# One reader for two PSUM banks: merged maxima and exponentials, and a third pair of W2 tiles split early

## The chip, the core and the metric

The kernel runs on one core of a Trainium2 chip. Its engines are TensorE (PE in the profile, with its weight loads listed apart as PEld), VectorE (DVE), ScalarE (ACT), GpSimd (POOL) and SyncE (SP, which here only issues DMAs). Each engine takes its instructions in the order of the program and waits on semaphores. The metric is the device time of one execution in microseconds (us).

## What is computed

```python
x = A_x                                             # [1, 2048, 576], float32
g = sigmoid((x * gate_w).sum(-1, keepdims=True))
# a: attention, 32 heads of 18 dimensions
q, k, v = split(x @ wqkv)
p = softmax(einsum("bhqd,bhkd->bhqk", q, k) * 18 ** -0.5)
a = concat(p @ v) @ wo
# b: MLP, 576 -> 4608 -> 576
h = gelu(layernorm(x) @ w1 + b1)                    # tanh form
b = h @ w2 + b2
out = g * a + (1 - g) * b
```

## The kernel before

The program has three parts. An **entry stage** loads x, normalises and transposes it, multiplies it with `wqkv`, and starts on the attention's maxima. A **loop** of 512 steps follows: 32 units (a pair of heads times one half of the 2,048 queries), each with 16 chunks of 128 keys. The **end** multiplies the attention's output with `wo` and adds the MLP's part.

Most float32 matrices are split into a high and a low part that TensorE multiplies as fp32r, so that products keep float32 accuracy. Heads come in pairs: head 0 lies in rows 0 to 63 of the array, head 1 in rows 64 to 127, and two matmuls of 64 rows that follow each other run side by side.

Each step of the loop holds, in the order in which the Python code emits it:

- two **S pairs** (`s2`, L263): for each head one matmul (L271) of 128 keys against 512 queries into a PSUM bank of its own, and for each head one exponential on ScalarE (L275) from that bank into the probabilities' ring (`p`, `ring`).
- two **R pairs** (`s1_round`, L216), for a unit that comes more than one unit later: for each head one matmul (L226) of 128 queries against 512 keys into a bank of its own, and one maximum over the row on VectorE (L228), which the later exponentials of that unit subtract through two more rows of the matmul.
- every two or three steps, `pv` (L280): the matmuls of probabilities and values (L291) for these steps.
- between them, pieces of the **MLP** (`atom`, L743): its hidden product (L539, `h_pair`) and its output product (L627, `out_pair`). `turn_ends` cuts one `h_pair` or one `out_pair` into the gaps between two calls of `pv`; below such a stretch is called a turn.

PSUM has eight banks of 512 float32 columns. In the loop the scores use five of them in turn (`score_bank`, L117: three of the pool `ps_s1` and two of `ps_s2`), the output of `pv` has one, and the MLP two. S and R pairs alternate, so the five banks go round through both. A matmul that reuses a bank waits for the instruction that read the bank last: ScalarE's exponential or VectorE's maximum.

The MLP's weights are read from the input once, split by ScalarE (L402 to L405, the high part) and GpSimd (through `pool_op`, L179, the low part), used, and stored to scratch; the later three blocks of 512 rows reload them. `prep` and `prep_w2` (L436, L450) ask for these splits ahead of time; `bg` holds them until their input is due (`LOADED`, a number of slots after the load was issued) and GpSimd's modelled queue is short. There are six W2 tiles (`room`), two for each pair of F chunks. Before, the entry stage asks for the first two pairs (`prep_w2(2)`, L688), and the others follow in the loop (L726).

Of the kernel before, what the change touches and what calls it, by code (L numbers as in the profile page):

```python
# [8 lines left out]
F32 = mybir.dt.float32  # L9
# [25 lines left out]
HALF = S // 2  # L35
NS1 = 3
LEAD = 4
# [29 lines left out]
def gated_mix_kernel(ctx: ExitStack, tc: tile.TileContext, x, wqkv, wo, w1, b1, w2, b2, gate_w, out):  # L67
# [34 lines left out]
    asm = ctx.enter_context(tc.tile_pool(name="asm", bufs=2))  # L102
    ps_s1 = ctx.enter_context(tc.tile_pool(name="ps_s1", bufs=NS1, space=PSUM))
    ps_o = ctx.enter_context(tc.tile_pool(name="ps_o", bufs=1, space=PSUM))
    QA = [att.tile([P, HALF], F32R, name=f"qa{i}") for i in range(3)]
# [5 lines left out]

    def psum(pool):
        return pool.tile([P, TB], F32, name="ps")

    ring = [0]

    def score_bank():  # L117

        ring[0] += 1
        if not looped[0]:  # L120
            return psum(ps_s1 if ring[0] % (NS1 + 1) < NS1 else ps_o)
        return psum(ps_s1 if ring[0] % (NS1 + 2) < NS1 else ps_s2)

# [92 lines left out]
    def s1_round(u, r):  # L216


        t, kb = (r % 8, r // 8) if u in (0, NU - 3) else divmod(r, 4)
        if r == 0:  # L220
            M4[u] = asm.tile([P, 2, 8, 4], F32, name="m4")
        qa, ka = QA[u % 3], KA[unit(u)[0] % 2]
        for h in range(2):
            r0 = 64 * h
            ps = score_bank()
            nc.tensor.matmul(ps, qa[r0:r0 + 54, t * P:(t + 1) * P], ka[r0:r0 + 54, kb * TB:(kb + 1) * TB],  # L226
                             start=True, stop=True)
            nc.vector.tensor_reduce(M4[u][:, h, t, kb:kb + 1], ps, axis=AX.X, op=ALU.max)  # L228

# [33 lines left out]
    def s2(u, kc, qb):  # L263
        qa, ka = QA[u % 3], KA[unit(u)[0] % 2]
        n = u * NT + kc
        if n < 2 and qb == 0:
            RING.insert(n, pp.tile([P, 2, 2, TB], F32, name="p"))
        ps = [score_bank() for _ in range(2)]
        for h in range(2):
            r0 = 64 * h  # L270
            nc.tensor.matmul(ps[h], ka[r0:r0 + 56, kc * P:(kc + 1) * P], qa[r0:r0 + 56, qb * TB:(qb + 1) * TB],  # L271
                             start=True, stop=True)
        def exps():
            for h in range(2):
                nc.scalar.activation(p_of(n)[:, qb, h], ps[h], AF.Exp, scale=SCALE)  # L275
        return exps
# [3 lines left out]
    def pv(n, m):  # L280

        u, kc = divmod(n, NT)
        if kc == 0:
            OB[u] = psum(ps_o)
# [55 lines left out]
    def mlp():  # L340
# [26 lines left out]
        def load_w1(q):  # L367

            if (1, q) in LOADED or q >= NQ0:
                return  # L370
            LOADED[1, q] = slot[0] + LAND
            f0 = 2 * q * P
            raw = raw1(q)
            for h in range(2):
                src = w1[256 * h:256 * h + 256, f0:f0 + 2 * P].rearrange("(c p) n -> p c n", p=64)
                nc.sync.dma_start(raw[64 * h:64 * h + 64, 0:8].rearrange("p (c j) n -> p c (j n)", j=2), src)
            for h in range(2):
                for j in range(2):
# [135 lines left out]
        def h_pair(q, inner=False):  # L514
# [8 lines left out]
            del W1[q]  # L523
            ps = [psum(ps_w) for _ in range(2)]
            change = tb + 1 < NB and (q + 1) % NQ0 == 0
# [78 lines left out]
        def out_pair(i, t, acc):  # L604
# [3 lines left out]
            cs = [slice(nn * ND, (nn + 1) * ND) for nn in range(2)]  # L608
            ps = [psum(ps_w) for _ in range(2)]
            steps = 12 * size  # L610
# [77 lines left out]
        prep_w2(2)  # L688
        prep(2)
        yield 1  # L690
        Y[1] = big_tile()
# [18 lines left out]
        for i in range(n + 1):  # L710
# [3 lines left out]
            if i > 0:  # L714
# [55 lines left out]
    with ExitStack() as a:  # L770
        wpool = a.enter_context(tc.tile_pool(name="a_w", bufs=1, side="right"))
        sm = a.enter_context(tc.tile_pool(name="a_sm", bufs=2, side="right"))
        ps_a = a.enter_context(tc.tile_pool(name="ps_a", bufs=4, space=PSUM))

# [45 lines left out]
        def transposed(tb, c):  # L820
            ps = psum(ps_a)
# [67 lines left out]
        def stat_rows(tb):  # L889

            ps = psum(ps_a)
            nc.tensor.transpose(ps[:, :P], stp, ident)
# [46 lines left out]
        def qk_group(tb, mt):  # L939
            big = xT[tb]  # L940
            wh, wl = W_QK
            ms = slice(mt * P, (mt + 1) * P)
            ps = psum(ps_a)
            k = 0
# [14 lines left out]
        def v_group(tb, t, n, between=None):  # L959
# [3 lines left out]
            wh, wl = W_V  # L963
            ps = psum(ps_a)
            k = 0
# [38 lines left out]
        for tb in range(NB):  # L1004
            work = [(qk_group, (tb, mt)) for mt in (range(9) if tb < 2 else (4, 0, 1, 2, 3, 5, 6, 7, 8))] + [(v_group, (tb, t, n)) for t in range(4) for n in range(2)]
            for g, (fn, args) in enumerate(work):
# [35 lines left out]
                if tb == NB - 1:  # L1042
# [12 lines left out]
                    if g == 7:  # L1055
                        ps = psum(ps_a)
                        nc.tensor.transpose(ps[:, :NFC], b1r, ident[:NFC, :NFC])
# [19 lines left out]

    ps_s2 = ctx.enter_context(tc.tile_pool(name="ps_s2", bufs=2, space=PSUM))
    ps_w = ctx.enter_context(tc.tile_pool(name="ps_w", bufs=2, space=PSUM))
    cw = ctx.enter_context(tc.tile_pool(name="c_w", bufs=1, side="right"))  # L1080
# [9 lines left out]
    def out_proj():  # L1090
# [171 lines left out]
        for b in range(NB):  # L1262
# [6 lines left out]
            for t in range(4):  # L1269
# [6 lines left out]
                for n in range(2):  # L1276
                    cs = slice(n * ND, (n + 1) * ND)
                    ps = psum(ps_w)
                    k = 0
# [127 lines left out]
```

## Time and profile before

| | us |
|---|---|
| Median of 3 runs | 2239.05 (2237.3 to 2239.54) |
| The profiled execution | 2238.79, its span 2237.0 |
| Entry stage, to the first S pair | 216.4 |
| Granted TensorE clock, mean | 0.994 |

| In the loop and around it (whole run) | instructions | mean ns of one |
|---|---|---|
| Maxima on VectorE, L228 | 2048 | 684 |
| Exponentials on ScalarE, L275 | 1048 + 1000 | 597 and 596 |
| R matmuls, L226 | 2048 | 403 |
| S matmuls, L271 | 2048 | 421 |
| Hidden product, L539 | 3888 | 393 |
| Output product, L627 | 6912 in four groups | 294 to 299 |

A group's line reads: source line, engine, operation, out<-in by the program's names, the shape, the count, then busy time, mean of one in ns, and the engine's idle time just before these instructions with what ended most of it. A line of the timeline reads: start, length (from the first start to the last end of merged neighbours), engine, line, operation, names, shape, count, and in brackets the idle time before it. Two matmuls of a pair overlap, so a pair's length of 0.40 us to 0.50 us is not the sum of the two.

### The profile page before, as it was taken

The page shows a single profiled execution, that of the slowest core. Times are in us where ns is not written, and L with a number is a line of the kernel's source. Part 1 is how long each engine was busy: PE and PEld are TensorE (multiplying, and loading weights), DVE is VectorE, ACT ScalarE, POOL GpSimd, SP SyncE. Part 2 cuts the span into 40 slices and gives each one's busy share as a digit, 9 for nine tenths or more (in the row PEclk, how much of TensorE's full clock was granted, in tenths as well). Part 3 has the DMA queues.
Part 4 walks back from the last instruction along what each step waited for, and adds up shares of the span by engine and source line. Part 5 has one row for each costly group of instructions (what it writes and reads, how often), then busy time and mean ns, then how long its engine had stood idle before and what let it go on. Part 6 is the DMA issues. An engine that isn't in the chain of part 4 may idle for free.

```text
span 2237.0 us, 51358 instructions
## 1 busy us (share of the span) xinstructions
PE 2204.4 (99%) x20496; PEld 1620.0 (72%) x20496; DVE 1619.0 (72%) x2816; ACT 1418.5 (63%) x2636; POOL 1005.0 (45%) x1017
## 2 busy tenths in 40 slices
PE   8999999999999999999999999999999999999999
PEld 7877666767677777777767677777677777777768
DVE  6675766777777777777777777777777777777734
ACT  4323866767776666666765676666666666667672
POOL 4322765556554525434543452543535354254600
PEclk9999999999999999999999999999999999999999
DMA  8857646444453522342341533243344324323355
GB/s 265 273 205 240 216 149 191 148 152 157 145 166 120 181 101 97 125 138 94 125 138 58 171 142 111 91 141 125 107 131 156 118 85 150 110 91 124 124 171 167
DMA packets 162041, 324.36 MB, mean 145 GB/s; under 512 B 65830, under 2 KB 85218, under 8 KB 151074
## 3 DMA queue, kind: packets, MB, share of 16 engines
q1 hardware_dynamic: 159494, 317.61, 44.1%
q8 instruction: 161, 2.64, 0.5%
q10 hardware_dynamic: 2244, 3.45, 0.4%
q14 instruction: 78, 0.64, 0.1%
q0 software_dynamic: 64, 0.02, 0.0%
HBM read 228.62 MB, written 96.69 MB: 145 GB/s over the span
## 4 chain that ended last, share of the span: by engine, by line
PE 86%; DMA 4%; DVE 4%; POOL 2%; issue 2%; SPq 1%; ACT 1%; POOLq 0%; ACTq 0%; DVEq 0%
PE ps L291 19%; PE ps L627 19%; PE ps L539 18%; PE ps L271 12%; PE ps L226 10%; PE ps L947 3%; PE ps L1284 2%; DVE m L228 2%; DMA x<-in_B_w_dram 1%; PE ps L968 1%; POOL zz L179 1%; POOL w L179 1%; DMA bt<-b_scr 1%; SPq L380 1%; DMA x<-ot_scr 0%
## 5 line engine op out<-in xcount | busy, mean ns | idle before, releaser
L228 DVE TENSOR_REDUCE m<-ps 128x1 f32<-128x512 f32 x2048 | 1302.5, 684 | 450.7 <-PE ps L226 428.8
L275 ACT ACTIVATE p<-ps 128x512 f32<-128x512 f32 x1048 | 567.5, 597 | 305.8 <-PE ps L271 277.3
L275 ACT ACTIVATE ring<-ps 128x512 f32<-128x512 f32 x1000 | 542.4, 596 | 273.1 <-PE ps L271 263.7
L539 PE MATMUL ps<-big,w 64*128 64x512 f32 x3888 | 612.7, 393 | 0.2 <-issue 0.2
L179 POOL TENSOR_SCALAR zz<-zz 128x512 f32<-128x512 f32 x288 | 178.2, 619 | 726.3 <-ACT zz L599 670.9
L271 PE MATMUL ps<-qa,ka 56*128 56x512 f32 x2048 | 474.2, 421 | 6.7 <-ACT ring L275 3.0
L226 PE MATMUL ps<-ka,qa 54*128 54x512 f32 x2048 | 461.1, 403 | 7.4 <-DVE m L228 7.3
L539 PEld LDWEIGHTS ps<-big,w 64*128 64x128 f32 x3888 | 412.1, 187 | 51.4 <-DMA big<-y_scr 0.5
L179 POOL TENSOR_TENSOR zz<-zz,z 128x512 f32<-128x512 f32 x288 | 371.2, 1289 | 24.0
L271 PEld LDWEIGHTS ps<-qa,ka 56*128 56x128 f32 x2048 | 220.8, 185 | 198.2 <-DVE m L228 124.0
L627 PE MATMUL ps<-w,hh 64*128 64x288 f32 x2752 | 317.9, 296 | 1.2 <-DMA w<-w_scr 1.2
L627 PEld LDWEIGHTS ps<-w,hh 64*128 64x128 f32 x2752 | 277.8, 188 | 15.7 <-POOL zz L179 1.0
L226 PEld LDWEIGHTS ps<-ka,qa 54*128 54x128 f32 x2048 | 245.9, 185 | 39.0 <-DVE m L228 14.2
L291 PE MATMUL ps<-p,vt 128*32 128x512 f32 x1968 | 240.7, 597 | 0.0
L627 PE MATMUL ps<-w,big 64*128 64x288 f32 x2496 | 234.0, 294 | 3.4 <-ACT w L405 2.5
L627 PE MATMUL ps<-w,hl 64*128 64x288 f32 x1376 | 233.1, 294 | 0.0
L291 PE MATMUL ps<-ring,vt 128*32 128x512 f32 x1872 | 231.3, 596 | 0.0
L627 PEld LDWEIGHTS ps<-w,big 64*128 64x128 f32 x2496 | 218.7, 188 | 13.9 <-ACT w L405 2.8
L179 POOL TENSOR_TENSOR w<-x,w 128x1024 fp32r<-128x1024 f32 (+1 forms) x72 | 101.3, 1429 | 211.7 <-ACT w L402 120.2
L627 PEld LDWEIGHTS ps<-w,hl 64*128 64x128 f32 x1376 | 159.3, 187 | 0.2
L291 PEld LDWEIGHTS ps<-p,vt 128*32 128x32 f32 x1968 | 54.5, 109 | 116.3 <-issue 107.9
L291 PEld LDWEIGHTS ps<-ring,vt 128*32 128x32 f32 x1872 | 52.5, 109 | 115.1 <-issue 115.1
(126 smaller groups left out, 1715.8 us busy)
## 6 DMA issues: line engine op xcount, KB each, us to landing
w<-w_scr SPq DMA_DIRECT2D x54, 1152.0 KB
w<-w_scr SPq DMA_DIRECT2D x108, 576.0 KB
w_scr<-w SPq DMA_DIRECT2D x18, 1152.0 KB
w_scr<-w SPq DMA_DIRECT2D x36, 576.0 KB
qa<-qk_scr SPq DMA_DIRECT2D x192, 72.0 KB
ka<-qk_scr SPq DMA_DIRECT2D x84, 144.0 KB
x<-in_B_w_dram SPq DMA_DIRECT2D x36, 288.0 KB
qk_scr<-hh SPq DMA_DIRECT2D x36, 256.0 KB
```

What stands on the lines that cost most here:

```text
L179: fn(*args, **kw)
L226: nc.tensor.matmul(ps, qa[r0:r0 + 54, t * P:(t + 1) * P], ka[r0:r0 + 54, kb * TB:(kb + 1) * TB], start=True, stop=True)
L228: nc.vector.tensor_reduce(M4[u][:, h, t, kb:kb + 1], ps, axis=AX.X, op=ALU.max)
L271: nc.tensor.matmul(ps[h], ka[r0:r0 + 56, kc * P:(kc + 1) * P], qa[r0:r0 + 56, qb * TB:(qb + 1) * TB], start=True, stop=True)
L275: nc.scalar.activation(p_of(n)[:, qb, h], ps[h], AF.Exp, scale=SCALE)
L291: nc.tensor.matmul(OB[u][r:r + 32, :], v[:, k, 19 * h:19 * h + 32], p_of(c)[:, qb, h, :], start=(k == 0), stop=(k == NT - 1))
L380: nc.sync.dma_start(raw[64 * h:64 * h + 64, 8 + j], w1[512:576, f1:f1 + P])
L539: mm = nc.tensor.matmul(ps[nn], w_[r, 2 * c + nn if c < 4 else 8], y, start=(k == 0), stop=(k == 26))
L627: mm = nc.tensor.matmul(ps[nn][:, :ND], h_[r, tok], w_[p_][r, cs[nn]], start=(k == 0), stop=(k == steps - 1))
L947: nc.tensor.matmul(ps, w_[:, c, ms], big[:, s_, :], start=(k == 0), stop=False)
L968: nc.tensor.matmul(ps[:, :ND], big[:, s_, tok], w_[:, c, cs], start=(k == 0), stop=False)
L1284: nc.tensor.matmul(ps[:, :ND], OT[b][2][:, s_, tok], w_part(w_, c)[:, cs], start=(k == 0), stop=(k == 13))
```

## The change

All PSUM is now one tile `PS` of eight banks, and tables say which banks a use goes round through: in the loop "s" is 0 to 4, "w" (the MLP) 6 and 7, "o" (`pv`) 5. `score_banks` takes two banks at once and tells whether they lie side by side. If so, one VectorE instruction takes both heads' maxima and one ScalarE instruction both heads' exponentials; if not, there are two as before. With five banks the pairs are (0,1), (2,3), (4,0), (1,2), (3,4): every fifth pair is read by two instructions. In the entry stage "s" is (0, 1, 2, 5), so every second pair is.

```diff
-    ps_s1 = ctx.enter_context(tc.tile_pool(name="ps_s1", bufs=NS1, space=PSUM))
-    ps_o = ctx.enter_context(tc.tile_pool(name="ps_o", bufs=1, space=PSUM))
+    PS = ctx.enter_context(tc.tile_pool(name="ps", bufs=1, space=PSUM)).tile([P, 8, TB], F32, name="ps")
...
+    BANKS = {"s": (0, 1, 2, 5), "a": (3, 4, 6, 7), "o": (5,), "w": (6, 7)}
+    given = {}
+    def bank(use):
+        given[use] = given.get(use, -1) + 1
+        return BANKS[use][given[use] % len(BANKS[use])]
+    def score_banks():
+        pair = (bank("s"), bank("s"))
+        if pair[1] == pair[0] + 1:
+            return [PS[:, b] for b in pair], [(slice(0, 2), PS[:, pair[0]:pair[1] + 1])]
+        return [PS[:, b] for b in pair], [(slice(h, h + 1), PS[:, b:b + 1]) for h, b in enumerate(pair)]
...
+        ps, reads = score_banks()
         for h in range(2):
             r0 = 64 * h
-            ps = score_bank()
-            nc.tensor.matmul(ps, qa[r0:r0 + 54, t * P:(t + 1) * P], ka[r0:r0 + 54, kb * TB:(kb + 1) * TB],
+            nc.tensor.matmul(ps[h], qa[r0:r0 + 54, t * P:(t + 1) * P], ka[r0:r0 + 54, kb * TB:(kb + 1) * TB],
                              start=True, stop=True)
-            nc.vector.tensor_reduce(M4[u][:, h, t, kb:kb + 1], ps, axis=AX.X, op=ALU.max)
+        for hs, banks in reads:
+            nc.vector.tensor_reduce(M4[u][:, hs, t, kb], banks, axis=AX.X, op=ALU.max)
...
-            for h in range(2):
-                nc.scalar.activation(p_of(n)[:, qb, h], ps[h], AF.Exp, scale=SCALE)
+            for hs, banks in reads:
+                nc.scalar.activation(p_of(n)[:, qb, hs], banks, AF.Exp, scale=SCALE)
...
+    BANKS["s"] = (0, 1, 2, 3, 4)
+    given["s"] = -1
```

The second part concerns W2: the entry stage asks for a third pair of tiles, a load that is issued in the loop counts as landed four slots later than before, and at a block's end the reloads are one slot apart, no longer two.

```diff
-            LOADED[1, q] = slot[0] + LAND
+            LOADED[1, q] = slot[0] + LAND + 4 * looped[0]
...
-            LOADED[2, c] = slot[0] + LAND
+            LOADED[2, c] = slot[0] + LAND + 4 * looped[0]
...
-        def prep_w2(upto):
+        def prep_w2(upto, apart=2):
...
-                    late += 2
+                    late += apart
...
         prep_w2(2)
         prep(2)
+        prep_w2(3)
...
-                    prep_w2(first_of[i] + seq[i][2] + 2 * (seq[i][0] == 0 and not last_of(i)))
+                    prep_w2(first_of[i] + seq[i][2] + 2 * (seq[i][0] == 0 and not last_of(i)), 1 if last_of(i) else 2)
```

TensorE's instructions stand in the same order before and after. On VectorE, early in the loop, twelve R pairs stand between an eviction of the hidden product (`z`) and the end of a unit's maxima (`nm`). Before:

```order
L564 TENSOR_SCALAR z<-ps,b1t 128x512
L228 TENSOR_REDUCE m_2125<-ps 128x1 x16
L564 TENSOR_SCALAR z<-ps,b1t 128x512
L228 TENSOR_REDUCE m_2125<-ps 128x1 x8
L235 TENSOR_REDUCE nm<-m_2125 128x16
```

and now, at the same place:

```order
L569 TENSOR_SCALAR z<-ps,b1t 128x512
L233 TENSOR_REDUCE m_1951<-ps 128x2
L233 TENSOR_REDUCE m_1951<-ps 128x1 x2
L233 TENSOR_REDUCE m_1951<-ps 128x2 x4
L233 TENSOR_REDUCE m_1951<-ps 128x1 x2
L233 TENSOR_REDUCE m_1951<-ps 128x2
L569 TENSOR_SCALAR z<-ps,b1t 128x512
L233 TENSOR_REDUCE m_1951<-ps 128x2 x3
L233 TENSOR_REDUCE m_1951<-ps 128x1 x2
L240 TENSOR_REDUCE nm<-m_1951 128x16
```

Nothing has moved past anything else; of 12 pairs here nine have one reduction with two results (128x2) and three still have two. On ScalarE, behind an eviction of the hidden product (`z`) early in the loop, before:

```order
L565 ACTIVATE z<-ps,b1t 128x512
L275 ACTIVATE ring_2367<-ps 128x512 x2
L599 ACTIVATE zz<-z 128x512 x2
L402 ACTIVATE w_2947<-x 128x1152
L403 ACTIVATE w_2947<-x 128x128
L275 ACTIVATE ring_2367<-ps 128x512 x2
L275 ACTIVATE ring_2371<-ps 128x512 x4
L275 ACTIVATE p<-ps 128x512 x2
```

and now:

```order
L570 ACTIVATE z<-ps,b1t 128x512
L280 ACTIVATE ring_2161<-ps 128x1024
L604 ACTIVATE zz<-z 128x512 x2
L407 ACTIVATE w_2622<-x 128x1152
L408 ACTIVATE w_2622<-x 128x128
L280 ACTIVATE ring_2161<-ps 128x512 x2
L280 ACTIVATE ring_2165<-ps 128x1024 x2
L280 ACTIVATE p<-ps 128x1024
```

Again the order is the same, and an exponential now has 1,024 columns wherever the pair's banks are neighbours. On SP's queue, at the change from the entry stage to the loop (`v_scr` is a store of the entry, `x<-in_B_w` a load of raw weights, `w_scr` a store of split ones), before:

```order
L982 DMA v_scr<-vt_111 128x780
L376 DMA x<-in_B_w_dram 64x4x256 x2
L380 DMA x<-in_B_w_dram 64x128 x4
L414 DMA w_scr<-w_2453 128x2304
```

and now:

```order
L987 DMA v_scr<-vt_109 128x780
L391 DMA x<-in_B_w_dram 128x576 x2
L419 DMA w_scr<-w_2184 128x1152
L381 DMA x<-in_B_w_dram 64x4x256 x2
L385 DMA x<-in_B_w_dram 64x128 x4
L419 DMA w_scr<-w_2234 128x2304
```

Two loads of W2 and a store of a split W2 tile (128x1152) have moved ahead of the next W1 load; the store of the other tile follows later.

More of the change, by code (lines that the diff above doesn't have):

```diff
@@ L35 @@
 HALF = S // 2
-NS1 = 3
 LEAD = 4
@@ L110, in gated_mix_kernel, with psum @@
     oe = att.tile([P, TB], F32, name="oe")
[L112 to L122, printed above, removed]
+    BANKS = {"s": (0, 1, 2, 5), "a": (3, 4, 6, 7), "o": (5,), "w": (6, 7)}
[3 more added lines that the diff above has]
+        return BANKS[use][given[use] % len(BANKS[use])]
+    def psum(use):
+        return PS[:, bank(use)]
+    def score_banks():
[3 more added lines that the diff above has]
+        return [PS[:, b] for b in pair], [(slice(h, h + 1), PS[:, b:b + 1]) for h, b in enumerate(pair)]
     def big_tile():
@@ L267, in s2 @@
             RING.insert(n, pp.tile([P, 2, 2, TB], F32, name="p"))
-        ps = [score_bank() for _ in range(2)]
+        ps, reads = score_banks()
         for h in range(2):
@@ L283, in pv @@
         if kc == 0:
-            OB[u] = psum(ps_o)
+            OB[u] = psum("o")
         v = v_of(unit(u)[0])
@@ L523, in h_pair @@
             del W1[q]
-            ps = [psum(ps_w) for _ in range(2)]
+            ps = [psum("w") for _ in range(2)]
             change = tb + 1 < NB and (q + 1) % NQ0 == 0
@@ L608, in out_pair @@
             cs = [slice(nn * ND, (nn + 1) * ND) for nn in range(2)]
-            ps = [psum(ps_w) for _ in range(2)]
+            ps = [psum("w") for _ in range(2)]
             steps = 12 * size
@@ L772, in gated_mix_kernel @@
         sm = a.enter_context(tc.tile_pool(name="a_sm", bufs=2, side="right"))
-        ps_a = a.enter_context(tc.tile_pool(name="ps_a", bufs=4, space=PSUM))
         qkstack = ExitStack()
@@ L820, in transposed @@
         def transposed(tb, c):
-            ps = psum(ps_a)
+            ps = psum("a")
             for t in range(4):
@@ L889, in stat_rows @@
         def stat_rows(tb):
-            ps = psum(ps_a)
+            ps = psum("a")
             nc.tensor.transpose(ps[:, :P], stp, ident)
@@ L942, in qk_group @@
             ms = slice(mt * P, (mt + 1) * P)
-            ps = psum(ps_a)
+            ps = psum("a")
             k = 0
@@ L963, in v_group @@
             wh, wl = W_V
-            ps = psum(ps_a)
+            ps = psum("a")
             k = 0
@@ L1055, in gated_mix_kernel @@
                     if g == 7:
-                        ps = psum(ps_a)
+                        ps = psum("a")
                         nc.tensor.transpose(ps[:, :NFC], b1r, ident[:NFC, :NFC])
@@ L1075, in gated_mix_kernel @@
                     run_due()
-    ps_s2 = ctx.enter_context(tc.tile_pool(name="ps_s2", bufs=2, space=PSUM))
-    ps_w = ctx.enter_context(tc.tile_pool(name="ps_w", bufs=2, space=PSUM))
+    BANKS["s"] = (0, 1, 2, 3, 4)
+    given["s"] = -1
     cw = ctx.enter_context(tc.tile_pool(name="c_w", bufs=1, side="right"))
@@ L1277, in out_proj @@
                     cs = slice(n * ND, (n + 1) * ND)
-                    ps = psum(ps_w)
+                    ps = psum("w")
                     k = 0
```

## The prediction

> **What bounds the kernel now.** I read the page's first part, then the groups, then the timeline of TensorE (PE) beside VectorE (DVE) and ScalarE (ACT), because the change touches the two engines that empty PSUM and leaves TensorE's order of matmuls as it is.
>
> ```profile
> span 2237.0 us, 51358 instructions
> PE 2204.4 (99%) x20496; PEld 1620.0 (72%) x20496; DVE 1619.0 (72%) x2816; ACT 1418.5 (63%) x2636; POOL 1005.0 (45%) x1017
> ```
>
> TensorE is busy for 99% of the span; VectorE and ScalarE have room. Less work on those two is therefore worth nothing by itself. What counts is only whether TensorE waits for them, and for that the idle column of the groups is the place.
>
> ```profile
> L228 DVE TENSOR_REDUCE m<-ps 128x1 f32<-128x512 f32 x2048 | 1302.5, 684 | 450.7 <-PE ps L226 428.8
> L275 ACT ACTIVATE p<-ps 128x512 f32<-128x512 f32 x1048 | 567.5, 597 | 305.8 <-PE ps L271 277.3
> L271 PE MATMUL ps<-qa,ka 56*128 56x512 f32 x2048 | 474.2, 421 | 6.7 <-ACT ring L275 3.0
> L226 PE MATMUL ps<-ka,qa 54*128 54x512 f32 x2048 | 461.1, 403 | 7.4 <-DVE m L228 7.3
> L627 PE MATMUL ps<-w,big 64*128 64x288 f32 x2496 | 234.0, 294 | 3.4 <-ACT w L405 2.5
> L539 PE MATMUL ps<-big,w 64*128 64x512 f32 x3888 | 612.7, 393 | 0.2 <-issue 0.2
> ```
>
> The score matmuls (L271 for the exponentials, L226 for the maxima) idle for 6.7 + 7.4 = 14.1 us in the whole run. That is all that an earlier release of banks could give back. The more telling question is how near the banks are to being late. A hand-over shows it:
>
> ```profile
> 374.83 0.68 DVE L228 TENSOR_REDUCE m<-ps 128x1 f32<-128x512 f32 x1
> 375.56 0.18 PEld L271 LDWEIGHTS ps<-qa,ka 56*128 56x128 f32 x1 [1.09 <-DVE m L228]
> 375.57 0.50 PE L271 MATMUL ps<-qa,ka 56*128 56x512 f32 x1 [0.76 <-DVE m L228]
> ```
>
> The reduction ends at 375.51, the waiting weight load starts 0.05 us later, and its matmul ends at 376.07: **0.55 us** from the end of the reader to the end of the matmul that reuses the bank. TensorE stands still meanwhile.
>
> **The change part by part.** *The merged instructions.* The ring has five banks and each pair of scores takes two. The second bank of a pair was the first bank of the pair two places earlier, which is the previous pair of the same kind (S for exponentials, R for maxima). Before, that bank was free after the first, single reader. Now, in four pairs of five, it is free only when one reader of 1,024 columns has finished both. How long is that reader? No row has it; the nearest are copies and subtractions of several widths:
>
> ```profile
> L818 DVE TENSOR_TENSOR wv<-p,wv 128x1440 fp32r<-128x1440 f32 x1 | 1.7, 1653 | 0.0
> L818 DVE TENSOR_TENSOR wqk<-p,wqk 128x864 fp32r<-128x864 f32 x1 | 1.1, 1058 | 0.1
> L817 ACT ACTIVATE wv<-p 128x1440 fp32r<-128x1440 f32 x2 | 2.8, 1400 | 1.9 <-DMA p<-in_A_wqkv_dram 1.9
> L817 ACT ACTIVATE wqk<-p 128x864 fp32r<-128x864 f32 x1 | 0.9, 917 | 0.0
> 1011.46 1.29 DVE L228 TENSOR_REDUCE m<-ps 128x1 f32<-128x512 f32 x2 [3.02 <-PE ps L226]
> 1000.54 1.09 ACT L275 ACTIVATE p<-ps 128x512 f32<-128x512 f32 x2
> ```
>
> VectorE: (1653 − 1058) / 576 = 1.03 ns a column, so 684 + 512 x 1.03 = 1,213 ns; I take **1.22**. ScalarE: (1400 − 917) / 576 = 0.84, so 597 + 429 = 1,026 ns; I take **1.03**. Two singles in a row take 1.29 and 1.09, not twice 0.68 and 0.60, because they overlap. So merging saves only some 0.06 us a pair, on engines that have room. Upper ends: no saving, 1.29 and 1.09. Lower ends: twice the interval between starts, 2 x (1.29 − 0.68) = 1.22 and 2 x (1.09 − 0.60) = 0.98.
>
> The new rule follows. A reader starts 0.04 us after its matmul: the exponentials above start at 1000.54, and the first matmul of their pair runs from 1000.10 (below) for some 0.40 us. From the end of a merged pair's matmuls to the end of the next pair of its kind there must be 0.04 + 1.22 + 0.55 = **1.81 us for R** and 0.04 + 1.03 + 0.55 = **1.62 us for S**. Now look at what the order of the program leaves, in a turn with the hidden product (L539) between the pairs:
>
> ```profile
> 1000.10 0.50 PE L271 MATMUL ps<-qa,ka 56*128 56x512 f32 x2
> ...
> 1001.04 0.49 PE L226 MATMUL ps<-ka,qa 54*128 54x512 f32 x2
> 1001.28 0.48 PE L271 MATMUL ps<-qa,ka 56*128 56x512 f32 x2
> ...
> 1002.48 0.46 PE L226 MATMUL ps<-ka,qa 54*128 54x512 f32 x2
> ...
> 1003.65 0.50 PE L226 MATMUL ps<-ka,qa 54*128 54x512 f32 x2
> ...
> 1004.82 0.52 PE L226 MATMUL ps<-ka,qa 54*128 54x512 f32 x2
> ```
>
> Ends are start plus length. The S pair after the one that ends at 1000.60 ends at 1001.76, but may not before 1000.60 + 1.62 = 1002.22: 0.46 late. R: 1001.53 + 1.81 = 1003.34 against 1002.94 + 0.46: in time. The next R needs 1003.40 + 1.81 = 1005.21 against 1004.15 + 0.46: 0.60 more. The next needs 1007.02 against 1005.34 + 1.06: 0.62 more. Counting from the loop's first pair, S at 1001.28 and R at 1004.82 are the split fifths, and their successors go free. The turn loses **1.68 us**. TensorE works in order, so nothing behind makes this up. An output turn (L627):
>
> ```profile
> 1694.44 0.50 PE L271 MATMUL ps<-qa,ka 56*128 56x512 f32 x2
> 1695.18 0.40 PE L226 MATMUL ps<-ka,qa 54*128 54x512 f32 x2
> 1695.81 0.40 PE L271 MATMUL ps<-qa,ka 56*128 56x512 f32 x2
> 1696.44 0.41 PE L226 MATMUL ps<-ka,qa 54*128 54x512 f32 x2
> 1697.07 0.41 PE L271 MATMUL ps<-qa,ka 56*128 56x512 f32 x2
> 1698.10 0.93 PE L226 MATMUL ps<-ka,qa 54*128 54x512 f32 x2
> ...
> 1700.26 0.40 PE L226 MATMUL ps<-ka,qa 54*128 54x512 f32 x2
> ...
> 1701.52 0.43 PE L226 MATMUL ps<-ka,qa 54*128 54x512 f32 x2
> ```
>
> In the same way: 0.35 (S at 1695.81), 0.19, 0.16, then 0.18 (R at 1700.26) and 0.52 (R at 1701.52): **1.40 us**. There are 3888 / 54 = 72 hidden turns and 27 groups x 4 = 108 output turns: 72 x 1.68 + 108 x 1.40 = 272 us. These two turns are a little worse than most, since the split fifth moves. The same walk over all pairs of the loop,
>
> ```profile
> L271 PEld LDWEIGHTS ps<-qa,ka x2048: 182/183/327, 216.4 to 2185.5; 56*128 56x128 f32 x187
> ```
>
> gives 117 us in hidden turns and 131 in output turns, 248 together. Applied to the single readers it gives 3 where it should give 0, so I take **+245**. With the lower ends of the durations the walk gives 229, with the upper 286.
>
> [...]
>
> *Cross waits.* A merged reader also waits for the other engine's earlier reader of the same bank; the matmul that filled the bank had waited for that already, so I cost it at nothing (upper end one step of the sequencer, 0.05 us as above, for each of some 1,600 merged readers if none is hidden: 80 us).
>
> *The third W2 pair.* Its two loads, two ACT copies and two POOL subtractions move from the loop's start into the entry stage, past the queues of SP and POOL there. What they cause now:
>
> ```profile
> 376.39 0.68 ACT L405 ACTIVATE w<-x 128x576 fp32r<-128x576 f32 x1 [3.98 <-DMA x<-in_B_w_dram]
> ```
>
> ScalarE stands for 3.98 us before a late tile, with the exponentials queued behind it. On TensorE such waits are in the 3.4 us of L627 and in the 3.0 that L271 idles behind `ACT ring`: 6.4 us at most. In the entry the copies cost at most 2 x 0.68 on ScalarE if uncovered. The later due time in the loop (LAND) and the closer reloads (`apart`) act on the same kind of wait; I put all of this at **−6**, between +1.4 and −17.5 (all of 14.1 + 3.4).
>
> **Sum.** The profiled execution took 2,238.8 (span 2,237.0 and 1.8 around it), 0.3 under the median of 2,239.05. 2,238.8 + 245 − 6 = **2,478 us**.
>
> **Rivals.** *A, it pays as meant (faster, 5%).* If the second matmul did not have to wait for the whole merged reader, the 14.1 us of waits would shrink and W2 would give its 6: 2,219. It decides at the spacing: R ends lie 1.19 to 1.41 apart in the first turn, so the reader would have to release a bank within 1.25 − 0.59 = 0.66 us, a single reduction's time. The hand-over rows speak against it: the weight load starts after the reader's end. *B, only the dense turns pay (14%).* If output turns with pairs some 1.7 us apart were the rule and lost 0.2 each, the sum is 72 x 1.68 + 108 x 0.2 − 6 = 137: 2,375. The turn at 1695 speaks against it, with pairs 1.26 apart. *C, the change does not do what it says (4%):* PSUM is now one tile, and if readers of different banks waited for each other, S and R would run in series, 1.03 + 1.22 + 2 x 0.04 = 2.33 us for each of 1,024 S-R rounds, 2,386 us for the loop alone against some 1,970 now: 2,650. The diff's bank-by-bank slices speak against it. *D, gains and stalls cancel (3%):* 2,239.
>
> **How the numbers follow.** The forecast holds 74%. The range reaches down to B, and up to the upper durations with a quarter of the cross waits' upper end (2,239 + 286 − 6 + 20): 2,370 to 2,540. Faster by over 0.2% (4.5 us, about what a measurement of this kernel can tell from no change) 5%, the same 3%, slower 92%.
>
> **What would show it.** Right: TensorE's idle time before L276 and L230 (the new numbers of L271 and L226) rises from 14 to over 150 us, ended by VectorE more than by ScalarE; rows of one merged reduction near 1.22 and of one exponential near 1.03; R ends never less than about 1.8 us apart behind a merged pair; VectorE's busy time down by some 60 us only. Wrong: R pairs that end 1.3 us apart behind a merged reduction, or a merged reduction near 0.8.

## The result and the profile after

| | us | ratio to before, 95% interval |
|---|---|---|
| Before, six runs beside the changed kernel | 2239.3 (2236.77 to 2246.03) | |
| The changed kernel, six runs | 2496.48 (2495.69 to 2498.99) | 1.1147, 1.1131 to 1.1163 |
| Its profiled execution, the span | 2494.1 | |

The change makes the kernel 257 us slower; the forecast was 2,478, with a range of 2,370 to 2,540. The line numbers move: the R matmul is now L230 and its maximum L233, the S matmul L276 and its exponential L280, the hidden product L544, the output product L632. First the head of the page after:

```profile
span 2494.1 us, 51087 instructions
PE 2380.2 (95%) x20496; PEld 1597.5 (64%) x20496; DVE 1584.2 (64%) x2009; ACT 1377.3 (55%) x1817; POOL 1006.0 (40%) x1017
```

VectorE runs 807 instructions fewer than before and is busy for 35 us less, ScalarE 819 fewer and 41 us less. Neither was the bound. The groups by shape, of the changed kernel:

```profile
L233 DVE TENSOR_REDUCE m<-ps 128x2 f32<-128x1024 f32 x807 | 987.8, 1224 | 636.1 <-PE ps L230 542.2 <-PE ps L276 47.5 <-ACT p L280 14.9
L280 ACT ACTIVATE p<-ps 128x1024 f32<-128x1024 f32 x420 | 430.5, 1026 | 363.8 <-PE ps L276 319.2 <-PE ps L296 23.3 <-DVE m L233 9.5
L230 PE MATMUL ps<-ka,qa 54*128 54x512 f32 x2048 | 699.7, 422 | 91.6 <-DVE m L233 89.6
L276 PE MATMUL ps<-qa,ka 56*128 56x512 f32 x2048 | 630.7, 430 | 8.9 <-ACT ring L280 1.9 <-ACT p L280 1.6
L230 PEld LDWEIGHTS ps<-ka,qa 54*128 54x128 f32 x2048 | 327.4, 184 | 278.0 <-DVE m L233 259.0 <-issue 2.0 <-DVE st L915 0.4
L632 PE MATMUL ps<-w,big 64*128 64x288 f32 x2496 | 271.0, 297 | 0.0
```

And of the kernel before the one row of this view that the prediction did not show, the weight loads of the R matmuls:

```profile
L226 PEld LDWEIGHTS ps<-ka,qa 54*128 54x128 f32 x2048 | 245.9, 185 | 39.0 <-DVE m L228 14.2 <-issue 1.6 <-DMA qa<-qk_scr 0.4
```

A merged maximum takes 1,224 ns and a merged exponential 1,026 ns. TensorE's idle time before score matmuls is now 91.6 + 8.9 = 100.5 us, from 14.1. That is far less than the 257 us lost, and the page even says that TensorE is busy for 2,380 us, from 2,204, with the same matmuls. L230 alone went from 461 to 700 us of busy time while the mean length of one went only from 403 to 422 ns. Busy time counts a stretch with two overlapping matmuls once: before, 2,048 x 403 ns, which is 825 us, made 461 us of busy time, and now 2,048 x 422 ns, which is 864, make 700. Matmuls that overlapped before now stand apart, and the stretches add up to more. The weight loads (PEld) tell it better: those of L230 stood idle behind VectorE's maxima for 14.2 us before and for 259.0 now.

One place of the changed kernel's timeline shows a whole round of it, R matmuls (PE), merged maxima (DVE) and weight loads (PEld) in order of time:

```profile
1117.44 0.39 PE L230 MATMUL ps<-ka,qa 54*128 54x512 f32 x1
...
1117.94 1.23 DVE L233 TENSOR_REDUCE m<-ps 128x2 f32<-128x1024 f32 x1 [0.97 <-PE ps L276]
...
1119.01 0.72 PE L230 MATMUL ps<-ka,qa 54*128 54x512 f32 x2
...
1119.22 0.18 PEld L230 LDWEIGHTS ps<-ka,qa 54*128 54x128 f32 x1 [0.16 <-DVE m L233]
...
1119.83 1.23 DVE L233 TENSOR_REDUCE m<-ps 128x2 f32<-128x1024 f32 x1 [0.67 <-PE ps L230]
...
1121.11 0.18 PEld L230 LDWEIGHTS ps<-ka,qa 54*128 54x128 f32 x1 [0.19 <-DVE m L233]
...
1121.11 0.49 PE L230 MATMUL ps<-ka,qa 54*128 54x512 f32 x1
```

The first R pair ends at 1117.83, its merged reader at 1119.17, the weight load for the second matmul of the next R pair starts at 1119.22, and that pair ends at 1119.73; the following one ends at 1121.60. The R pairs end 1.90 and 1.87 us apart, and both times the weight load before the later pair's last matmul had waited for VectorE. The pair of 0.72 us (x2) is one whose second matmul came late; before, such a pair took 0.40 to 0.50.

### The profile page after: what moved, and what is told of

Its sections match the earlier page's. It is cut to its first block, busy times and chain, and to the rows that moved or that the text cites. A ratio compares the mean times of both kernels' runs of the same rounds, so it can differ in the third digit from the quotient of the medians.

```text
span 2494.1 us, 51087 instructions
## 1 busy us (share of the span) xinstructions
PE 2380.2 (95%) x20496; PEld 1597.5 (64%) x20496; DVE 1584.2 (64%) x2009; ACT 1377.3 (55%) x1817; POOL 1006.0 (40%) x1017
## 4 chain that ended last, share of the span: by engine, by line
PE 75%; DVE 16%; ACT 4%; DMA 2%; issue 2%; DVEq 0%; POOL 0%; SPq 0%; ACTq 0%
PE ps L296 18%; PE ps L230 14%; DVE m L233 14%; PE ps L544 12%; PE ps L632 12%; PE ps L276 11%; PE ps L952 3%; ACT p L280 2%; PE ps L1289 2%; ACT ring L280 2%; PE ps L973 1%; DMA w<-w_scr 1%; DMA out_dram<-res 0%; DMA bt<-b_scr 0%; DMA p<-in_A_wqkv_dram 0%
## 5 line engine op out<-in xcount | busy, mean ns | idle before, releaser
L233 DVE TENSOR_REDUCE m<-ps 128x2 f32<-128x1024 f32 (+1 forms) x1241 | 1264.5, 1035 | 721.6 <-PE ps L230 616.4
L280 ACT ACTIVATE p<-ps 128x1024 f32<-128x1024 f32 (+1 forms) x628 | 543.6, 883 | 442.9 <-PE ps L276 387.3
L230 PE MATMUL ps<-ka,qa 54*128 54x512 f32 x2048 | 699.7, 422 | 91.6 <-DVE m L233 89.6
L280 ACT ACTIVATE ring<-ps 128x1024 f32<-128x1024 f32 (+1 forms) x601 | 519.3, 881 | 443.0 <-PE ps L276 401.5
L544 PE MATMUL ps<-big,w 64*128 64x512 f32 x3888 | 696.2, 400 | 0.0
L276 PE MATMUL ps<-qa,ka 56*128 56x512 f32 x2048 | 630.7, 430 | 8.9 <-ACT ring L280 1.9
L230 PEld LDWEIGHTS ps<-ka,qa 54*128 54x128 f32 x2048 | 327.4, 184 | 278.0 <-DVE m L233 259.0
L544 PEld LDWEIGHTS ps<-big,w 64*128 64x128 f32 x3888 | 448.6, 186 | 58.3 <-DMA big<-y_scr 0.5
L276 PEld LDWEIGHTS ps<-qa,ka 56*128 56x128 f32 x2048 | 316.8, 184 | 254.4 <-issue 130.4
L632 PE MATMUL ps<-w,hh 64*128 64x288 f32 x2752 | 378.3, 299 | 0.0
L632 PEld LDWEIGHTS ps<-w,hh 64*128 64x128 f32 x2752 | 300.3, 186 | 7.5 <-ACTq L491 0.4
L632 PE MATMUL ps<-w,hl 64*128 64x288 f32 x1376 | 287.4, 292 | 0.0
L632 PE MATMUL ps<-w,big 64*128 64x288 f32 x2496 | 271.0, 297 | 0.0
L632 PEld LDWEIGHTS ps<-w,big 64*128 64x128 f32 x2496 | 229.8, 186 | 5.6
L632 PEld LDWEIGHTS ps<-w,hl 64*128 64x128 f32 x1376 | 205.8, 185 | 0.0
```

Of the source, the lines that this page charges most:

```text
L230: nc.tensor.matmul(ps[h], qa[r0:r0 + 54, t * P:(t + 1) * P], ka[r0:r0 + 54, kb * TB:(kb + 1) * TB], start=True, stop=True)
L233: nc.vector.tensor_reduce(M4[u][:, hs, t, kb], banks, axis=AX.X, op=ALU.max)
L280: nc.scalar.activation(p_of(n)[:, qb, hs], banks, AF.Exp, scale=SCALE)
L544: mm = nc.tensor.matmul(ps[nn], w_[r, 2 * c + nn if c < 4 else 8], y, start=(k == 0), stop=(k == 26))
L632: mm = nc.tensor.matmul(ps[nn][:, :ND], h_[r, tok], w_[p_][r, cs[nn]], start=(k == 0), stop=(k == steps - 1))
```

## The experiments

Each ran beside the kernel before on the same chip. All times are medians. The median of the kernel before lay between 2,235.85 and 2,239.3 us from one group of runs to the next, so that a difference of two runs from different groups is uncertain by some 3 us.

| run | us | ratio to before, 95% interval |
|---|---|---|
| singles | 2218.76 | 0.9927, 0.9912 to 0.9941 |
| max_only | 2484.89 | 1.1111, 1.1095 to 1.1128 |
| exp_only | 2332.97 | 1.0431, 1.0413 to 1.0448 |
| second_first | 2562.82 | 1.1465, 1.1448 to 1.1482 |
| max_half | 2228.71 | 0.9954, 0.9940 to 0.9967 |
| merge_far | 2226.06 | 0.9947, 0.9934 to 0.9959 |
| w2_only | 2220.65 | 0.9918, 0.9904 to 0.9931 |
| one_tile | 2237.80 | 0.9993, 0.9982 to 1.0003 |
| w2_third | 2234.66 | 0.9988, 0.9977 to 0.9998 |
| w2_land | 2225.83 | 0.9939, 0.9925 to 0.9952 |
| w2_land_third | 2219.98 | 0.9917, 0.9904 to 0.9931 |
| w2_undone | 2511.55 | 1.1220, 1.1205 to 1.1236 |

### Is it the merged readers?

Theory: the merged readers hold a pair's first bank too long. Rival: the single tile of all banks, or the W2 part, costs. The changed kernel with every bank read by itself:

```diff
-        if pair[1] == pair[0] + 1:
+        if False:
```

> All as in the changed kernel (one PSUM tile, five banks, W2 part), but every bank has its own reader again. Theory H (a merged reader holds the first bank of its pair until both are read): the loss is gone, and only the W2 part is left, about 2,239 - 6 = 2,233 us, between 2,220 and 2,245. Rival T (the one PSUM tile and its extra waits between VectorE and ScalarE cost the time): it stays above 2,400 us.

2,218.76: all of the loss is gone, and 0.7% more than that, so that the time is a little under the expected range. The merged readers cost 278 us over it (274 if each of the two is counted from the kernel before that ran beside it), and what else is in the change gains. The rows of this run that answer to those above:

```profile
span 2217.6 us, 51398 instructions
L230 PE MATMUL ps<-ka,qa 54*128 54x512 f32 x2048 | 455.4, 402 | 6.4 <-DVE m L233 6.2
L230 PEld LDWEIGHTS ps<-ka,qa 54*128 54x128 f32 x2048 | 241.6, 184 | 37.5 <-DVE m L233 12.9 <-issue 2.0 <-DVE st L915 0.4
```

TensorE's 259 us behind the maxima are 12.9 again.

### Which of the two?

Only the maxima merged, and only the exponentials, by a flag of `score_banks` that the caller sets. Shown is `max_only`, where `s2` asks for single readers; in `exp_only` `s1_round` does:

```diff
-    def score_banks():
+    def score_banks(merge=True):
-        if pair[1] == pair[0] + 1:
+        if merge and pair[1] == pair[0] + 1:
...
-        ps, reads = score_banks()
+        ps, reads = score_banks(False)
```

> Only the maxima are merged; the exponentials have one reader for each bank. H: behind a merged reduction the next R pair must end 1.88 us later (0.11 + 1.22 + 0.55, the 0.11 as the changed kernel's trace shows it); the walk over the pairs gives +259 of the +279 that it gives for both, so nearly all the loss remains: about 2,475 us (2,450 to 2,495). Rival E (both merged readers cost about alike): half of the loss, about 2,365 us.

> Only the exponentials are merged. H: S pairs must end 1.61 us apart; the walk gives +120 by itself, though it adds only some 20 on top of merged maxima: about 2,345 us (2,320 to 2,365). Rival E (half of the loss each): about 2,365 us; rival S (the shares add up, so what merged maxima leave is small): about 2,250 us.

Over the single readers the maxima alone cost 266 us, the exponentials alone 114, both together 274 to 278. The two don't add up: a TensorE that waits behind a maximum gives the exponentials time (the S matmuls' weight loads stand 126.6 us behind exponentials with the exponentials alone merged, and 45.1 + 36.9 = 82.0 us in the changed kernel). The prediction's walk over the pairs has this in it; with the start of VectorE's merged readers mended as told below, it gives 259, 120 and 279. The view of the waits (engine, tile and line, what it waited for, us in total, times, the longest) puts the loss where the theory has it. With the maxima merged:

```profile
PEld ps L230 <- DVE m L233: 300.1, 520, 2.0
```

With the exponentials merged:

```profile
PEld ps L276 <- ACT p L280: 64.9, 199, 0.6
PEld ps L276 <- ACT ring L280: 61.7, 183, 0.7
```

### Is it the instruction or the release?

The rival now is that a reader of 1,024 columns is slow as such. Two runs tell it apart. In the first nothing is merged, but the second head's bank is read first, so that the first bank comes free after two readers:

```diff
-        if pair[1] == pair[0] + 1:
+        if False:
...
-        for hs, banks in reads:
+        for hs, banks in reads[::-1]:
```

(the last line in `s1_round` and in `s2`)

> No merged instruction at all, but of each pair the second head's bank is read first and the first head's bank last. H: the first bank comes free after two readers in a row (0.04 + 1.29 for the maxima, 0.04 + 1.09 for the exponentials), later than with a merged one, in all pairs and not four of five; the walk gives +336, so slower than the changed kernel: about 2,550 us (2,510 to 2,580). Rival M (the merged instruction itself is what costs, by its width or its two-bank access): as fast as with single readers, about 2,235 us.

2,562.82, so 344 us over the same readers in the other order. Not one instruction is merged here, and it is worse than the change. In the second the maxima stay merged but are short; each reads only the first 256 columns of both banks, and the other half of the columns is left out of the maxima (of the split pairs' maxima too):

```diff
-            nc.vector.tensor_reduce(M4[u][:, hs, t, kb], banks, axis=AX.X, op=ALU.max)
+            nc.vector.tensor_reduce(M4[u][:, hs, t, kb], banks[:, :, :TB // 2], axis=AX.X, op=ALU.max)
```

(with the exponentials single, as in the run of the maxima alone)

> The changed kernel with the maxima merged as in it, but each merged maximum reads only the first 256 of the 512 columns of both banks (the other columns are left out of the maxima), and with every exponential on its own. If what costs is the time from the last matmul of a pair to the release of both of its banks, the shorter reader (near 0.68 us instead of 1.22) brings that to about 0.11 + 0.68 + 0.55 = 1.34 us, which few pairs are closer than: about 2,240 us (2,225 to 2,260), beside 2,219 with all readers single. If merging costs by its form (one instruction that waits for both matmuls and for the other engine, whatever its length), the time stays where merged maxima alone put it, 2,485 us.

2,228.71: of the 266 us that merged maxima cost, all but 7 to 10 are gone. The groups of this run:

```profile
L233 DVE TENSOR_REDUCE m<-ps 128x2 f32<-128x512 f32 x807 | 557.5, 691 | 774.5 <-PE ps L230 671.6 <-PE ps L276 42.4 <-ACT p L280 33.2
L230 PEld LDWEIGHTS ps<-ka,qa 54*128 54x128 f32 x2048 | 279.8, 185 | 51.3 <-DVE m L233 26.2 <-issue 3.6 <-DVE st L915 0.4
```

The same 807 readers of two banks, with the same waits, now take 691 ns. Over the records of this run, R pairs behind such a reader end 1.347 us apart or more in nineteen cases of twenty, against 1.878 in the changed kernel: the difference, 0.53, is the reader's (1,224 − 691 = 533 ns). What costs is the time until both banks are free.

### Where merging costs little

Merged only where the block of `pv` follows, whose matmuls need no score bank:

```diff
+    far = [False]
...
-        if pair[1] == pair[0] + 1:
+        if far[0] and pair[1] == pair[0] + 1:
...
-            exps = s2(u, kc, 0)
...
-            full = step - begun[0] >= span[0]
+            full = far[0] = step - begun[0] >= span[0]
+            exps = s2(u, kc, 0)
...
             half_round(step, gap if step else GAPS - 1, full or step == 0)
+            far[0] = False
```

> The changed kernel, but merged only where it stands right before the block of probability matmuls (one S pair and one R pair of every block, where their banks lie side by side: four in five); all other banks have readers of their own. The next pair that writes the banks of such a pair comes only after that block, over 3.6 us later, so that a release that is 0.6 us later makes nothing wait. If merging costs only through the time to the first bank's release: 2,219 us (2,214 to 2,226), as with all readers single. If merged readers cost wherever they stand, in proportion to their number (about a quarter of those of the changed kernel, which cost 278 us over single readers): near 2,290 us.

2,226.06, at the edge of the first range. The profile counts the merged readers:

```profile
L235 DVE TENSOR_REDUCE m<-ps 128x2 f32<-128x1024 f32 x138 | 167.9, 1217 | 0.0
L282 ACT ACTIVATE p<-ps 128x1024 f32<-128x1024 f32 x77 | 79.0, 1026 | 54.8 <-PE ps L278 33.7 <-PE ps L298 13.6 <-DVE m L235 4.9
L282 ACT ACTIVATE ring<-ps 128x1024 f32<-128x1024 f32 x72 | 73.9, 1026 | 32.2 <-PE ps L278 24.1 <-PE ps L298 5.1 <-DVE m L235 2.8
```

138 + 149 = 287 of them, of the 1,626 in the changed kernel, cost 4 to 7 us over the single readers; 278 x 287 / 1,626 = 49 would be their share by number. So the place decides most of it. The blocks are shorter than expected: by the records, `pv` holds TensorE for 1.9 us behind 119 of these readers, for 2.8 behind 118 and for 3.6 behind 50 only. That is still enough, since the pair that needs the banks ends 2.8 us or more after the merged pair, and only 5 of the 287 times as little as 0.55 to 0.57 us after its reader. Where the remaining 4 to 7 us come from stays open. And nothing is gained, even here.

### What the rest of the change brings

Everything but the merged readers gained 17 us. The W2 part and the one tile of banks were tried apart (`w2_only` is the kernel before with the W2 part; `one_tile` is `singles` with the W2 part undone), and then the W2 part's edits:

```diff
+        prep_w2(3)
...
-            LOADED[1, q] = slot[0] + LAND
+            LOADED[1, q] = slot[0] + LAND + 4 * looped[0]
```

`w2_third` has the first of these, `w2_land` the second (for W2's tiles too), `w2_land_third` both; the closer reloads (`apart`) are in `w2_only` alone.

> The kernel before, with its own pools of banks and single readers, and of the change only the W2 part (third pair split in the entry, later due time of weight loads in the loop, closer reloads). With single readers and everything else of the change the time was 2,218.8 us against 2,235.9 before. If the W2 part is all of that gain: 2,219 us (2,214 to 2,225). If the one tile of banks brings it: 2,236 us.

> The other half: the one tile of banks with every reader single, and the W2 part undone. If the W2 part is all of the gain: 2,236 us (2,230 to 2,242), and the two stalls of the entry near 315 and 376 us of the trace, after each of which the granted clock was 0.77 to 0.84, are there again. If the one tile brings it: 2,219 us.

> The kernel before and, of the W2 part, only the third pair split in the entry; due times and distances of reloads as before. If the stalls of the entry are the gain and the earlier split removes them: 2,219 us, as with the whole W2 part. If the later due time or the closer reloads matter as much: half-way, 2,225 to 2,231 us. If they bring all of it: 2,236 us.

> The kernel before, and of the W2 part only the later due time of the copies of loaded weights (four slots later in the loop). The stalls near 315 and 376 us of the trace of before begin with a copy on ScalarE that waits for its load. If the later due time takes them away alone: 2,220 us, as with the whole W2 part. If it needs the third pair split early as well: 2,228 to 2,236 us.

> The kernel before with the later due time and the third pair split in the entry, without the closer reloads at a block's end. If the closer reloads are of no account: 2,220 us, as with the whole W2 part; if they bring what the third pair alone did not: 2,230 us or more.

The W2 part alone gives 2,220.65, 17.9 us under its before; the one tile gives 2,237.80, no difference. Of the edits, the early split alone is worth 4 us (2,238.56 to 2,234.66), the later due time alone 13 (2,239.08 to 2,225.83), both 19, which is all; the closer reloads are of no account. So the due time, not the early split, does most. Of the three cases named for `w2_third` the last is the nearest; `w2_land` came out between its two.

Why, the windows of the loop's first 300 us show. (The loop begins at 216.4 us, so the expectations' "stalls of the entry" lie in the loop.) Columns: stretch, its length, busy time and count of PE, PEld, DVE, ACT, POOL, then the granted clock, DMA share and GB/s. The kernel before:

```profile
310.00:320.00 10.00, 6.59 (x58) 3.99 (x51) 2.67 (x5) 4.83 (x9) 6.45 (x6) 0.82 0.86 302
320.00:330.00 10.00, 10.00 (x86) 7.50 (x84) 7.14 (x13) 5.70 (x11) 7.36 (x9) 0.84 0.21 86
370.00:380.00 10.00, 7.06 (x63) 3.52 (x61) 4.87 (x8) 5.55 (x11) 2.68 (x3) 0.89 0.87 307
380.00:390.00 10.00, 10.00 (x77) 7.76 (x79) 5.27 (x10) 5.47 (x11) 9.49 (x10) 0.77 0.66 209
480.00:490.00 10.00, 9.03 (x81) 6.14 (x77) 7.10 (x11) 4.98 (x10) 0.55 (x1) 1.00 0.84 258
490.00:500.00 10.00, 7.88 (x65) 5.83 (x67) 4.76 (x9) 6.43 (x12) 8.50 (x9) 0.83 0.92 316
220.00:2050.00 1830.00, 1809.35 (x17683) 1305.46 (x17681) 1369.82 (x2335) 1244.45 (x2303) 890.80 (x909) 0.99 0.42 133
```

The W2 part alone:

```profile
310.00:320.00 10.00, 10.00 (x107) 6.03 (x105) 7.51 (x14) 8.62 (x17) 6.52 (x6) 1.00 0.71 245
320.00:330.00 10.00, 9.68 (x80) 7.03 (x74) 7.52 (x14) 5.50 (x11) 7.71 (x9) 1.00 0.51 175
370.00:380.00 10.00, 9.94 (x94) 6.96 (x92) 7.16 (x12) 7.95 (x15) 7.64 (x9) 1.00 1.02 358
380.00:390.00 10.00, 9.95 (x95) 6.58 (x93) 7.79 (x15) 7.86 (x15) 4.93 (x4) 1.00 0.13 33
480.00:490.00 10.00, 10.00 (x88) 6.98 (x87) 7.43 (x14) 7.06 (x14) 8.55 (x10) 1.00 0.88 265
490.00:500.00 10.00, 10.00 (x110) 6.68 (x110) 7.56 (x14) 8.71 (x18) 5.70 (x6) 1.00 0.29 94
220.00:2050.00 1830.00, 1818.24 (x17839) 1312.23 (x17837) 1381.99 (x2359) 1252.61 (x2320) 896.33 (x916) 1.00 0.42 133
```

Before, TensorE stands idle for 3.41, 2.94 and 3.09 us at three places, and at each the granted clock falls to one half and stays there for a while (by its records for 6.83, 6.83 and 3.41 us, from 316.38, 377.82 and 493.88). With the W2 part all three dips are gone. The last rows tell what that is worth. From 220 to 2,050 us TensorE idles for 20.7 us before and for 11.8 with the W2 part, 8.9 less. By the records of the clock it ran at one half for 27.3 us of this stretch before and for 10.2 with the W2 part; half of the difference, 8.5 us, is an estimate of what the slow clock cost. Together that is 17.4 of the 17.9 us, though the two overlap a little, where TensorE idled while the clock was slow.

The edits divide the stalls between them. With the later due time alone the second and third are gone, and the first stays (TensorE idle for 4.0 us between 310 and 320). With the early split alone all three are there (1.9, 2.6 and 3.2 us in the stretches from 310, 370 and 480).

In each of the three ScalarE stood before a copy (L405) whose load had not landed. In the whole run it did so for 13.0 us in the kernel before, by its groups:

```profile
L405 ACT ACTIVATE w<-x 128x576 fp32r<-128x576 f32 x36 | 23.5, 685 | 13.0 <-DMA x<-in_B_w_dram 13.0
```

for 2.5 with the W2 part alone, and for 0.4 in the changed kernel, where the line is L410:

```profile
L405 ACT ACTIVATE w<-x 128x576 fp32r<-128x576 f32 x36 | 23.6, 687 | 2.6 <-DMA x<-in_B_w_dram 2.5
L410 ACT ACTIVATE w<-x 128x576 fp32r<-128x576 f32 x36 | 23.4, 680 | 0.4 <-DMA x<-in_B_w_dram 0.4
```

Last, the W2 part undone beside the merged readers (all its edits as before):

> The changed kernel with its merged readers, and the whole W2 part undone. With single readers the W2 part was worth 18 us (2,238.6 against 2,220.7 and the like). If it is worth as much beside the merged readers: 2,514 us (2,508 to 2,521), with the two stalls of the entry stage near 315 and 376 us. If TensorE's slower pace under the merged readers already gives the loads the time that they lacked: 2,497 to 2,503 us, and then the merged readers cost some 260 us over the kernel before rather than 278.

2,511.55, 15 us over the changed kernel. The W2 part is worth nearly as much there, and the merged readers cost 2,511.55 − 2,237.80 = 274 us where it is undone, 274 to 278 where it is in. The two parts hardly touch each other. The stalls came at other places than expected: the clock of this run falls to one half at 331 and 400 us, not near 315 and 376. The fastest kernels of the study, `singles`, `w2_only` and `w2_land_third`, keep single readers and take the W2 part, or two edits of it: 2,219 to 2,221 us, 0.7 to 0.8% under before.

## Why the prediction was right, point by point

**The bound.** TensorE was the bound, and less work on VectorE and ScalarE was worth nothing: shown by `second_first`, in which VectorE is busy for much the same time as in `singles` (1,633 and 1,617 us) and the kernel takes 344 us more, and by `max_half`, in which it is busy for 1,045 us only and nothing is gained over `singles`. Breaking the merged instructions up again is worth 274 to 278 us.

**The readers' lengths.** Taken as 1.22 and 1.03; measured 1.224 and 1.026.

**Release to end of the matmul, 0.55.** Over the records of the changed kernel, where an R pair ends within 0.65 us of the reader that it waited for, the median is 0.549. It held.

**The rule for S, 1.62.** Of 818 S pairs behind a merged reader the closest end 1.61 apart. It held.

**The rule for R, 1.81: too small.** Of the 787 R pairs behind a merged reader, ninety-nine in a hundred end 1.877 apart or more (median 1.888, the closest 1.833). Nearly the whole difference is the reader's start. VectorE's merged readers start 0.107 us after the matmul's end, not 0.04, in the median of the records. In the timeline above, 1119.73 to 1119.83. This is the term that failed: the prediction saw that a merged reader also waits for the other engine and wrote "I cost it at nothing", with an upper end of 0.05 us a reader. The two waits come as two steps. The view of one line's instructions (count, then duration min/median/max in ns, and the first and last start) shows them on VectorE's sequencer, in the changed kernel:

```profile
L233 DVEq EVENT_SEMAPHORE  x983: 21/21/21, 221.2 to 2376.0; - x197
```

and in the kernel before:

```profile
L228 DVEq EVENT_SEMAPHORE  x1: 1512/1512/1512, 217.0 to 217.0; - x1
```

983 semaphore instructions now stand on the line of the 1,241 maxima, where one stood for 2,048. Nearly all of them wait for TensorE; the reduction behind them then waits for ScalarE, which has long been done, and still starts 0.07 us later. The same trace holds the comparison: of a split pair, the first reader, which has both waits, starts at 0.106, and the second, which waits for TensorE alone, at 0.037. Most of ScalarE's merged readers have both waits too, but in the other order, with TensorE's on the instruction itself, and start at 0.037. No kernel was run with the order of the two waits turned round, but the other traces hold both orders. In `exp_only`, where no maximum is merged, 465 maxima with the semaphore instruction ahead start at 0.107 and 78 without it at 0.038, so a reader need not span two banks to start late. And on ScalarE, in the kernel before, 331 exponentials whose semaphore instruction waits for TensorE and which themselves wait for ScalarE's own earlier work start at 0.097; 37 with a semaphore instruction ahead, but with a wait for TensorE on themselves, start at 0.037, as do 366 without one. (All medians are over readers whose engine stood idle.) That the order is the cause rests on these comparisons.

**The merged readers, +245.** 274 to 278 measured. The same walk over the pairs of before with 0.107 for R's start gives 282, less the 3 that it gives where it should give none: 279. So the mechanism and the walk were right, and the term that was too small is the merged reader's second wait: 0.07 us a round in place of nothing, 34 us in all by the walk.

**The W2 part, −6.** −15 beside merged readers, −18 beside single ones, near the far end that was stated (−17.5). The prediction looked at the waits' own microseconds, 6.4 at most. In these are the stall near 316 us (the 3.4 of L627) and the longer part of the one near 491 (2.4 of the 3.0 behind `ACT ring`). The one near 376, of which it showed ScalarE's side, is missing: on TensorE it stands under other releasers, 1.4 us under `ACT p` and 1.6 under VectorE's maxima. And the prediction left out that the clock fell at these stalls (to one half for 6.83, 6.83 and 3.41 us), some 8.5 us of the loop by the estimate above.

**The sum.** 2,238.8 + 279 − 18 = 2,500, or 2,503 with −15; measured 2,496. The two misses, +29 to +33 and −9 to −12, have opposite signs; that the forecast's error is only 18 us is in part luck.

**The rivals.** A, that it pays as meant, and B, that only dense turns pay (2,375), fell by the result. C, that the readers of one tile wait for each other, fell by `one_tile`. D, no change, fell by the result.

**The tests named.** TensorE's idle rows were to pass 150 us and came to 100.5. This test was badly made: it asked the one column in which a longer wait can show as busy time. The others came out: lengths of readers, R ends never under 1.8 apart, and VectorE's busy time down a little only (35, not 60).

## What to carry to other kernels

Before merging two readers of buffers that go round, ask which buffer is needed first, and when: the first one's release moves from the end of its own reader to the end of both, and where the engine that waits was the bound, that was paid here with 274 to 278 us, while two short instructions in a row cost hardly more than one long one (1.29 against 1.22 us here). Count the waits of a merged instruction as well, since with a second engine to wait for, one that was long done, the maxima here started 0.107 us after their matmul in place of 0.037. And judge such a wait on the weight loads' idle time and on the distance between the ends of successive pairs, not on TensorE's busy share: here the R matmuls' weight loads went from 14.2 to 259.0 us behind VectorE, while TensorE's busy time rose from 2,204 to 2,380 us.

## What the runs showed of the hardware

**A stall of some 3 us cost about twice its idle time here, by estimate.** Finer windows of the kernel before, at its second stall:

```profile
374.00:380.00 6.00, 3.06 (x27) 1.96 (x25) 2.67 (x4) 3.14 (x6) 2.68 (x3) 0.82 0.97 345
380.00:384.00 4.00, 4.00 (x30) 4.00 (x31) 1.29 (x2) 2.49 (x6) 3.83 (x4) 0.50 0.78 229
384.00:387.00 3.00, 3.00 (x24) 1.06 (x23) 2.02 (x4) 0.80 (x2) 2.75 (x5) 0.89 1.01 339
387.00:390.00 3.00, 3.00 (x28) 2.70 (x28) 1.96 (x4) 2.18 (x4) 2.92 (x3) 1.00 0.16 51
```

And the last of the idle stretches, from the timeline:

```profile
379.74 0.79 PE L271 MATMUL ps<-qa,ka 56*128 56x512 f32 x1 [1.37 <-ACT p L275]
```

TensorE idles for 2.94 of the first 6 us, in three pieces of which none is over 1.4 us. The granted clock of the first three rows makes 6.8 us at one half, (0.18 x 6 + 0.50 x 4 + 0.11 x 3) / 0.5, and the clock's records put them in one piece, from 377.82 to 384.65: the clock fell behind the first two pieces, 0.76 and 0.82 us, and ahead of the last. Half of 6.8, some 3.4 us, is lost by estimate (2.7 if the last idle piece is left out of it), beside the 2.94.

In the loop of the kernel before, the clock's records hold five stretches at one half, 6.83, 6.83, 3.41, 3.41 and 6.83 us long, from 316.38, 377.82, 493.88, 592.87 and 1173.13. In the 3.41 us ahead of each (the length of the shortest) TensorE had idled for 2.27, 1.57, 1.66, 1.55 and 1.28 us, not always in one piece, as the second of them shows. No rule follows from this. In the changed kernel TensorE idles far longer in all (101 us of the loop, where before had 21), in pieces of under 1.5 us and up to 1.8 us within 3.41, and the mean granted clock is 1.000: none of those waits brought it down. What tells them from the five is not shown.

**Back-to-back readers overlapped here.** Two single maxima in a row take 1.29 us where one takes 0.684, and a merged one 1.224. So in this kernel no more than 0.07 us a pair was to be had of merging two maxima.
